# GLU pairs: the low-weight passes of the 64-channel rest as couples of 64-row matmuls

## Chip, cores and metric

The kernel runs on one core of a Trainium2 chip. The metric is the device time of one execution in microseconds (us); before the change it is 1588.62 us, the median of three runs.

## What is computed

A pre-norm block over one sequence of 2048 tokens with 576 channels, all in float32: layer norm, attention with 32 heads of 18 channels in which a token looks at itself and seven earlier tokens at distance 2, an output projection and a residual; then layer norm and a gated linear unit with 4608 hidden channels, and a second residual. The change lies in the gated unit:

```python
S, D, F = 2048, 576, 4608
h = x + attention(layernorm(x), wqkv) @ wo
y = layernorm(h)
g = einsum("bsd,df->bsf", y, w_gate)
u = einsum("bsd,df->bsf", y, w_up)
out = h + einsum("bsf,fd->bsd", sigmoid(g) * u, w_down)
```

## The kernel before

**Numbers in two parts.** Products run in a 32-bit format that TensorE reads with fewer bits (fp32r). So `split` (L104, L105) makes of each operand a high part (a rounded copy by ScalarE) and a low part (the remainder, by VectorE), and a product of 128 input channels is three passes: high weights by high and by low data, low weights by high data.

**576 channels.** They are four blocks of 128 channels and a rest of 64. The rest has tiles of its own, packed twice: the weights of the rest stand in rows 0 to 63 and again in rows 64 to 127. Of the data, rows 0 to 63 hold the high part and rows 64 to 127 the low part (`split_rest`, which subtracts in rows 64 to 127). So one pass with the high weights over 128 rows does high and low data at once; a second pass with the low weights over 128 rows does low weights by high data, and, in the other 64 rows, low by low. `rest` (L612 to L617) issues these two passes.

**Blocks and pairs.** The tokens are four blocks of 512. The 4608 hidden channels are 36 groups of 128. A group is worked out for two token blocks together by `pair`, which takes the gate and up products of both blocks as seven products in place of eight, with sums and differences of the operands (`a00`, `s2`, `s3` and so on for the data, `b00`, `t2`, `t3` and so on for the weights). Each product (`prod`, L603 to L610) covers 256 of the channels: two blocks of 128, three passes each, six matmuls of 128x128 weights by 512 columns. The rest of 64 channels isn't part of that scheme: it is added by four calls of `rest`, to gate and up of each block.

**Banks.** A pair works in three PSUM banks, b1, b2 and b3. Several products go into the same bank one after the other, and in between the bank's content is copied out (`s1`, `s2`, `s3`, by ScalarE) or added to what was copied (by VectorE), which the next product into this bank waits for. The three names rotate from pair to pair over three tiles of 512 columns; the third tile also serves background work (`bg_bank`) outside of the pairs.

**The order of work.** The run over the groups is a list of items: 14 groups singly for the first two token blocks, 22 as pairs, 14 singly for the other two blocks, 36 as pairs. Between the products of a pair, `between(i)` puts in units of the down-projection of earlier groups (`down_units`, L723, in the first pairs; `down_seven`, L785, in the last 36) and steps of background work: attention and projection of the later token blocks in the first pairs, operands for the down-projection in the last. Weights are loaded two groups ahead and split one group ahead (`weights`). A scheduler that knows priorities (`tc.high_priority`) sets the final order on each engine; a matmul can so move past neighbours that it doesn't depend on.

Of the kernel before, what the change touches and what calls it, by code (L numbers as in the profile page):

```python
# [17 lines left out]
AF = mybir.ActivationFunctionType  # L18
ALU = mybir.AluOpType
# [34 lines left out]
HC = 700  # L54
# [6 lines left out]
def kernel(ctx, tc, x, wqkv, wo, wmlp, out):  # L61
    nc = tc.nc
    dve, act, pool, pe, sp = nc.vector, nc.scalar, nc.gpsimd, nc.tensor, nc.sync
# [34 lines left out]
    def f32(ap):  # L98
        return ap.bitcast(F32)
# [3 lines left out]
    def split(hi, lo, src):  # L103
        act.activation(hi, src, AF.Copy)  # L104
        splits.append(dve.tensor_tensor(lo, src, f32(hi), ALU.subtract))  # L105

    def split_rest(t, src):
        act.activation(t, src, AF.Copy)
        dve.tensor_tensor(t[64:128], src[64:128], f32(t[64:128]), ALU.subtract)  # L109

    def pads(g):
        for e in range(2):
# [174 lines left out]
    def th_tile():  # L287
        return xt.tile([P, 5, TB], F32R, tag="th", bufs=3, name="th")

    def tl_tile():  # L290
        return xt.tile([P, 4, TB], F32R, tag="tl", bufs=4, name="tl")

    def x_half(raw, rest):
        t = tl_tile() if rest is None else th_tile()
        split(t[:, 0:2], t[:, 2:4], raw)
        if rest is not None:
            split_rest(t[:, 4], rest)
        return t


# [64 lines left out]
    def qkv_w(g, wr=None):  # L365
        w = saw.tile([P, 2, 5, NQ], F32R, tag="qw", bufs=2, name="qw")
        for c in range(5):
            if wr is None:
                ws = sas.tile([P, NQ], F32, tag="wst", bufs=3, name="ws")
                sp.dma_start(ws, wqkv[g][:, c * NQ:(c + 1) * NQ])  # L370
            else:
                ws = wr[:, c]
            with tc.high_priority(3 * HI if g == 0 else HI):
                split(w[:, 0, c], w[:, 1, c], ws)
        return w
# [63 lines left out]
    w = [qkv_w(0, raw_w(0))]  # L439
# [78 lines left out]
    X = {}  # L518
# [85 lines left out]
    def prod(ps, xx, w, n, first):  # L604
        wt, k0 = w[n]
        k = 0
        for c in range(2):
            for a, m in ((0, 0), (0, 2), (1, 0)):
                pe.matmul(ps, wt[:, a, k0 + c], xx[:, m + c], start=first and k == 0,  # L609
                          stop=k == 5, skip_group_check=True)  # L610
                k += 1

    def rest(ps, xx, w, n):
        wt, k0 = w[n]
        for a in range(2):
            pe.matmul(ps, wt[:, a, k0], xx[:, 4], start=False, stop=a == 1,  # L616
                      skip_group_check=True)  # L617

    gc_bufs = 3

    def halves(name, src):
# [13 lines left out]
    def b_tile(i):  # L635
        return gp.tile([P, TB], F32, name=f"b{i % 3 + 1}")
# [31 lines left out]
    added = [None]  # L668
    gated = [None]

    turn = [2]

    def pair(X, w, between, last):
        turn[0] += 1
        b1, b2, b3 = (b_tile(turn[0] + k) for k in range(3))
        s1, s2, s3 = s_tile(), s_tile(), s_tile()
        prod(b1, X["a00"], w, "b00", True)
        with tc.high_priority(HC):
            act.activation(s1, b1, AF.Copy)
        between(0)  # L680
        prod(b2, X["a01"], w, "b10", True)
        rest(b2, X["a01"], w, "g4")
        with tc.high_priority(HC):
            added[0] = dve.tensor_tensor(s1, s1, b2, ALU.add)
            act.activation(s1, s1, AF.Sigmoid)
        between(1)
        prod(b1, X["s2"], w, "t2", False)
        with tc.high_priority(HC):
            act.activation(s2, b1, AF.Copy)
        between(2)  # L690
        prod(b3, X["s3"], w, "t3", True)
        with tc.high_priority(HC):
            act.activation(s3, b3, AF.Copy)
        between(3)
        prod(b1, X["s1"], w, "t1", False)
        rest(b1, X["a11"], w, "u4")
        with tc.high_priority(HC):
            added[0] = dve.tensor_tensor(s3, s3, b1, ALU.add)  # L698
        between(4)
        prod(b3, X["a11"], w, "t4", False)  # L700
        rest(b3, X["a11"], w, "g4")
        with tc.high_priority(HC):
            added[0] = dve.tensor_tensor(s2, s2, b3, ALU.add)
            gated[0] = act.activation(s2, s2, AF.Sigmoid)
        between(5)
        prod(b1, X["s4"], w, "b11", False)
        rest(b1, X["s4"], w, "u4")
        with tc.high_priority(HC):
            last((s1, b1), (s2, s3))
        between(6)  # L710

# [157 lines left out]
    def operands(pp, p, Xn, names, a0, a1):  # L869
        if p == 0:  # L870
            a0 = pp.tile([P, 5, TB], F32, name="ar0")
            pool.dma_start(a0, xscr[0])
        s = [pp.tile([P, 2, TB], F32, name=f"rs{i}") for i in range(3)]
        rd = pp.tile([P, TB], F32, name="rd")
        if p == 1:
            for n in ("a00", "a01"):
                a = a0[:, 0:2] if n == "a00" else a0[:, 2:4]
                with tc.high_priority(HI):
                    Xn[n] = x_half(a, None if n == "a00" else a0[:, 4])
                yield  # L880
        raw = yield from sums(a0, a1, a1[:, 0:2] if p == 1 else a0[:, 0:2], *s, rd)
        for n in names:
            with tc.high_priority(HI):
                Xn[n] = x_half(*raw[n])
            yield
        return raw

# [15 lines left out]
    Xn = {}  # L903
# [35 lines left out]
    raw = None  # L939
# [170 lines left out]
    for c, (kind, p, f) in enumerate(items):  # L1110
        w, d = wc
        for b, late_c in ((0, NF + NSTD - 3), (1, NF + NSTD + 5)):
            if c == late_c:
                e, hf = BLOCKS[b]
                paced(ov[e, hf], hacc[b])
        skip = () if kind == "std" else (3,)
        by_seven = c >= NF + NSTD
        if c == NSTD:
            finish_bg()
            last_x = splits[-1]  # L1120
            bg = under_rest(getattr(last_x, "ins", last_x))
        if c == NF + NSTD:
            finish_bg()
            with tc.high_priority(HI):
                for n in ("s1", "a11"):
                    Xn[n] = x_half(*raw[n])
            X = Xn
            pp_stk.close()
            dw = ctx.enter_context(sb_pool("dw", "right"))
        if c + 1 < len(items):  # L1130
            wc = weights(items[c + 1][0], wg, c + 1 < NF + NSTD)
        if c + 2 < len(items):
            wg = load_gu(items[c + 2][2], n=WC if c + 2 < NF + NSTD else GU)
        hid = {}
        blocks = [p] if kind == "std" else [2 * p, 2 * p + 1]

        def last(h0, h1):
            hid[0] = hidden(*h0, "h0")
            hid[1] = hidden(*h1, "h1")

        if kind == "std":
            hid = single(X, w, p, late, twice)
        elif not by_seven:
            side = last_pair if c == NF - 1 else bg_step

            def between(i):
                if i in (4, 6):
                    units(2)
                side(i)

            pair(X, w, between, last)
        else:
            def between(i):
                nonlocal st, gc, gc_bufs, dk
                units(1)
                if c == NF + NSTD and i == 5:
                    assert not queue
                    st_stk.close()
                    gc_stk.close()
                    gc = gc_stk.enter_context(sb_pool("gc2"))  # L1160
                    st = st_stk.enter_context(sb_pool("st2"))
                    dk = dk_stk.enter_context(sb_pool("dk", "right"))
                    for n in ("s4h", "s4l", "s1h"):
                        dk.tile([P, TB], F32R, name=n)
                    gc_bufs = 2
                down_side(f, i)

            pair(X, w, between, last if f >= NF - NPL else last_sums(f))
            if f < NF - NPL:
                if f % 2:  # L1170
                    if f == 1:
                        queue.append(lag(LAG))
                    queue.append(seven())
                continue
            d = M[f]
        seg.append((hid, d))
        if len(seg) == 2:
            if by_seven and f == NF - NPL + 1:
                queue.append(load_tails())
            for b in blocks:  # L1180
                queue.append(down_std(seg, b, f // 2) if kind == "std" else
                             down_tail(seg, b, f == NF - 1) if by_seven else down_units(seg, b))
            seg = []
# [44 lines left out]
```

## Time and profile before

| | |
|---|---|
| timed runs, median of 3 | 1588.62 us (1587.64 to 1589.95) |
| profiled execution, first to last instruction | 1589.2 us |
| TensorE matmul busy (PE) | 1553.3 us, 98% |
| TensorE weight loads busy (PEld) | 1381.6 us, 87% |
| VectorE busy (DVE) | 1268.1 us, 80% |
| ScalarE busy (ACT) | 869.2 us, 55% |
| GpSimd busy (POOL) | 184.2 us, 12% |
| mean granted TensorE clock | 0.993 |

The profile is of one execution by itself, with no other time given for it than its span; it lies among the timed runs. Weight loads overlap matmuls, and the end of a matmul is modelled, so busy times of neighbouring matmuls overlap too: what a matmul costs in a dense stretch is read from the start of one to the start of the next. In the rows of the profile, a group has line, engine, operation, tiles written and read, shape (128\*128 is rows by columns of the weights), count, then busy time, mean length of one in ns, and idle time before. A row of the timeline has start, time, engine, line and count, with neighbours of one kind merged.

### The profile page before, as it was taken

What the parts mean: (1) busy time and instruction counts of PE and PEld (TensorE: products, weight loads), DVE (VectorE), ACT (ScalarE), POOL (GpSimd) and SP (SyncE); (2) the same over time, 40 slices, a digit from 0 to 9 for tenths busy, and PEclk for the clock granted to TensorE, in tenths of its full rate; (3) what the DMA queues carried; (4) which work ended last, traced back from release to release, by engine and by line L of the source; (5) the groups of instructions that cost most, each with busy time, mean ns of one, the idle gap of its engine ahead of it and who ended that gap; (6) DMA issues with size and microseconds to landing.
All of it is one profiled execution on the core that took longest, in us unless ns stands there. A gap on an engine that the chain in (4) does not pass through costs nothing.

```text
span 1589.2 us, 22383 instructions
## 1 busy us (share of the span) xinstructions
PE 1553.3 (98%) x8532; PEld 1381.6 (87%) x8532; DVE 1268.1 (80%) x1931; ACT 869.2 (55%) x1546; POOL 184.2 (12%) x230
## 2 busy tenths in 40 slices
PE   7999979999999999999989999999999999999998
PEld 6999968888888888888879988888888888888887
DVE  7999988959999999999546687876677776677755
ACT  4432234425555666656443255776677776677761
POOL 1000000011010001000101100122112112212210
PEclk9999999999999999999999999999999999999999
DMA  7664544346367565665764234899989999989983
GB/s 267 208 206 163 193 184 165 133 177 246 104 164 205 157 170 139 166 191 149 210 203 143 100 110 110 182 186 181 176 169 183 184 173 180 177 170 182 184 170 124
DMA packets 76892, 273.50 MB, mean 172 GB/s; under 512 B 8336, under 2 KB 14224, under 8 KB 75888
## 3 DMA queue, kind: packets, MB, share of 16 engines
q0 software_dynamic: 27792, 105.89, 36.3%
q1 hardware_dynamic: 41360, 146.06, 27.4%
q10 hardware_dynamic: 7632, 20.12, 3.3%
q8 instruction: 67, 1.10, 0.3%
q14 instruction: 41, 0.34, 0.1%
HBM read 145.88 MB, written 128.52 MB: 173 GB/s over the span
## 4 chain that ended last, share of the span: by engine, by line
PE 55%; issue 27%; POOL 7%; DVE 6%; DMA 4%; ACT 1%; SPq 0%; POOLq 0%; ACTq 0%; DVEq 0%
PE b L609 23%; PE dp L723 15%; POOL h L794 7%; PE acc L150 6%; PE b L616 4%; PE b L150 1%; PE bgp L150 1%; DMA wg<-in_wmlp_dram 1%; DVE pr L182 1%; DMA x<-tok 1%; DVE pr L208 1%; DVE lg L186 1%; PE acc L152 1%; DMA tail<-h 1%; PE acc L153 1%
## 5 line engine op out<-in xcount | busy, mean ns | idle before, releaser
L609 PE MATMUL b<-tl,w 128*128 128x512 f32 x1716 | 438.1, 395 | 9.1 <-ACT w L104 6.5
L609 PEld LDWEIGHTS b<-tl,w 128*128 128x128 f32 x1716 | 311.7, 189 | 66.5 <-ACT w L104 7.7
L609 PE MATMUL b<-th,w 128*128 128x512 f32 x1368 | 352.8, 393 | 0.4 <-DVE s L698 0.3
L609 PEld LDWEIGHTS b<-th,w 128*128 128x128 f32 x1368 | 249.8, 188 | 46.7 <-DVE s L698 0.7
L104 ACT ACTIVATE w<-wg 128x640 fp32r<-128x640 f32 (+2 forms) x197 | 117.0, 598 | 125.2 <-PE b L616 59.8
L791 ACT ACTIVATE ev<-dp 128x576 f32<-128x576 f32 x224 | 145.0, 647 | 61.8 <-PE dp L785 58.2
L616 PE MATMUL b<-th,w 128*128 128x512 f32 x572 | 177.0, 391 | 0.0
L794 POOL DMA_DIRECT2D h<-ev x128 | 110.2, 862 | 456.8 <-ACT ev L791 440.5
L105 DVE TENSOR_TENSOR w<-wg,w 128x640 fp32r<-128x640 f32 (+2 forms) x197 | 126.8, 649 | 38.7 <-ACT w L104 38.3
L150 PE MATMUL acc<-qw,th 128*128 128x432 f32 x512 | 155.7, 365 | 1.2 <-DVE th L109 0.9
L105 DVE TENSOR_TENSOR w<-tw,w 128x512 fp32r<-128x512 f32 x116 | 79.6, 687 | 81.1 <-ACT w L104 80.2
L616 PEld LDWEIGHTS b<-th,w 128*128 128x128 f32 x572 | 107.7, 188 | 23.1
L723 PE MATMUL dp<-d,h0h 128*128 128x288 f32 x640 | 119.0, 296 | 1.7 <-DVE tail L733 1.7
L723 PE MATMUL dp<-d,h1h 128*128 128x288 f32 x640 | 120.0, 297 | 0.0
L723 PEld LDWEIGHTS dp<-d,h0h 128*128 128x128 f32 x640 | 99.4, 189 | 5.5 <-DVE tail L733 2.0
L150 PEld LDWEIGHTS acc<-qw,th 128*128 128x128 f32 x512 | 97.2, 190 | 6.5 <-DVE th L109 1.1
L723 PEld LDWEIGHTS dp<-d,h1h 128*128 128x128 f32 x640 | 99.5, 190 | 2.9
L731 ACT ACTIVATE stage<-dp 128x576 f32<-128x576 f32 x96 | 61.7, 646 | 62.4 <-PE dp L723 62.3
L104 ACT ACTIVATE w<-tw 128x512 fp32r<-128x512 f32 x116 | 72.8, 628 | 41.3 <-PE b L609 40.9
L150 PE MATMUL acc<-qw,tl 128*128 128x432 f32 x256 | 92.8, 362 | 0.0
L384 ACT ACTIVATE ev<-acc 128x432 f32<-128x432 f32 x64 | 33.9, 531 | 104.4 <-PE acc L153 97.7
L182 DVE TENSOR_TENSOR pr<-kw,q 128x2304 f32<-128x2304 f32 x32 | 81.7, 2552 | 2.8 <-DMA kw<-k 2.6
(278 smaller groups left out, 2899.8 us busy)
## 6 DMA issues: line engine op xcount, KB each, us to landing
h<-ev POOLq DMA_DIRECT2D x96, 576.0 KB, 7.2
wg<-in_wmlp_dram SPq DMA_DIRECT2D x49, 928.0 KB, 5.2
h<-stage POOLq DMA_DIRECT2D x24, 1152.0 KB, 10.6
wg<-in_wmlp_dram SPq DMA_DIRECT2D x36, 640.0 KB, 4.1
kw<-k SPq DMA_DIRECT2D x16, 792.0 KB, 4.4
vw<-v SPq DMA_DIRECT2D x16, 792.0 KB, 5.5
wd<-in_wmlp_dram SPq DMA_DIRECT2D x18, 576.0 KB, 7.2
h<-ev POOLq DMA_DIRECT2D x32, 288.0 KB, 6.8
```

Of the source, the lines that this page charges most:

```text
L104: act.activation(hi, src, AF.Copy)
L105: splits.append(dve.tensor_tensor(lo, src, f32(hi), ALU.subtract))
L150: pe.matmul(ps[:, :n], a[:, c, js], m[:, c], start=k == 0, stop=False)
L152: pe.matmul(ps[:, :n], th[:, 4, js], wh[:, 4], start=False, stop=False)
L182: dve.tensor_tensor(pr, both(kw, u), q[:, us].unsqueeze(2).broadcast_to([P, 2, W, CG]), ALU.mult)
L384: act.activation(ev[:, :, j], ps[:, :NQ].rearrange("p (t c) -> p t c", t=3), AF.Copy)
L609: pe.matmul(ps, wt[:, a, k0 + c], xx[:, m + c], start=first and k == 0, stop=k == 5, skip_group_check=True)
L616: pe.matmul(ps, wt[:, a, k0], xx[:, 4], start=False, stop=a == 1, skip_group_check=True)
L723: pe.matmul(ps[:, i, :DH2], a[:, js], d[:, m, i * DH2:(i + 1) * DH2], start=k == 0, stop=k == n)
L731: act.activation(hv, ps, AF.Copy)
L791: act.activation(hs[:, k % 2], ps[:, :, :DH2], AF.Copy)
L794: pool.dma_start(hsev[:, u, k0:k + 1], hs[:, :k + 1 - k0], accum_op=ALU.add, max_dma_last_dim=8 * D)
```

## The change

The pass with the low weights needs 64 rows only, those that hold the high part of the data. `rest_two` takes two rests at a time: first the two passes with high weights over 128 rows, then the two passes with low weights, the first on rows 0 to 63 and the second on rows 64 to 127, into different banks. The second of the two always has the operand `a11`: for it the halves of the data are packed the other way round (`low=0`: low part in rows 0 to 63, high part in rows 64 to 127), so that its high part lies in the half that is used. In the second couple the half of rows 0 to 63 is `s4` and that of rows 64 to 127 `a11`.

So that two rests meet, the products of a pair stand in another order, and the four calls become two: gate of the first block with up of the second, and the two remaining ones at the end. The bank b3 is always the third tile now, and b1 and b2 change places from pair to pair.

```diff
-    def split_rest(t, src):
+    def split_rest(t, src, low=1):
         act.activation(t, src, AF.Copy)
-        dve.tensor_tensor(t[64:128], src[64:128], f32(t[64:128]), ALU.subtract)
+        r = slice(64 * low, 64 * low + 64)
+        dve.tensor_tensor(t[r], src[r], f32(t[r]), ALU.subtract)
...
+    def rest_two(top, bot, w):
+        for ps, xx, n in (top, bot):
+            wt, k0 = w[n]
+            pe.matmul(ps, wt[:, 0, k0], xx[:, 4], start=False, stop=False, skip_group_check=True)
+        for i, (ps, xx, n) in enumerate((top, bot)):
+            wt, k0 = w[n]
+            r = slice(64 * i, 64 * i + 64)
+            pe.matmul(ps, wt[r, 1, k0], xx[r, 4], start=False, stop=True, skip_group_check=True)
...
-    turn = [2]
+    turn = [0]
 
     def pair(X, w, between, last):
-        turn[0] += 1
-        b1, b2, b3 = (b_tile(turn[0] + k) for k in range(3))
+        turn[0] = 1 - turn[0]
+        b1, b3, b2 = b_tile(turn[0]), b_tile(2), b_tile(1 - turn[0])
         s1, s2, s3 = s_tile(), s_tile(), s_tile()
         prod(b1, X["a00"], w, "b00", True)
         with tc.high_priority(HC):
             act.activation(s1, b1, AF.Copy)
         between(0)
-        prod(b2, X["a01"], w, "b10", True)
-        rest(b2, X["a01"], w, "g4")
+        prod(b3, X["s3"], w, "t3", True)
         with tc.high_priority(HC):
-            added[0] = dve.tensor_tensor(s1, s1, b2, ALU.add)
-            act.activation(s1, s1, AF.Sigmoid)
+            act.activation(s3, b3, AF.Copy)
         between(1)
         prod(b1, X["s2"], w, "t2", False)
         with tc.high_priority(HC):
             act.activation(s2, b1, AF.Copy)
         between(2)
-        prod(b3, X["s3"], w, "t3", True)
-        with tc.high_priority(HC):
-            act.activation(s3, b3, AF.Copy)
+        prod(b2, X["a01"], w, "b10", True)
         between(3)
         prod(b1, X["s1"], w, "t1", False)
-        rest(b1, X["a11"], w, "u4")
+        rest_two((b2, X["a01"], "g4"), (b1, X["a11"], "u4"), w)
         with tc.high_priority(HC):
             added[0] = dve.tensor_tensor(s3, s3, b1, ALU.add)
+            added[0] = dve.tensor_tensor(s1, s1, b2, ALU.add)
+            act.activation(s1, s1, AF.Sigmoid)
         between(4)
         prod(b3, X["a11"], w, "t4", False)
-        rest(b3, X["a11"], w, "g4")
+        between(5)
+        prod(b1, X["s4"], w, "b11", False)
+        rest_two((b1, X["s4"], "u4"), (b3, X["a11"], "g4"), w)
         with tc.high_priority(HC):
             added[0] = dve.tensor_tensor(s2, s2, b3, ALU.add)
             gated[0] = act.activation(s2, s2, AF.Sigmoid)
-        between(5)
-        prod(b1, X["s4"], w, "b11", False)
-        rest(b1, X["s4"], w, "u4")
-        with tc.high_priority(HC):
             last((s1, b1), (s2, s3))
         between(6)
```

More of the change, by code (lines that the diff above doesn't have):

```diff
@@ L291, in tl_tile, with x_half @@
         return xt.tile([P, 4, TB], F32R, tag="tl", bufs=4, name="tl")
-    def x_half(raw, rest):
+    def x_half(raw, rest, low=1):
         t = tl_tile() if rest is None else th_tile()
@@ L296, in x_half @@
         if rest is not None:
-            split_rest(t[:, 4], rest)
+            split_rest(t[:, 4], rest, low)
         return t
@@ L883, in operands @@
             with tc.high_priority(HI):
-                Xn[n] = x_half(*raw[n])
+                Xn[n] = x_half(*raw[n], n != "a11")
             yield
@@ L1125 @@
                 for n in ("s1", "a11"):
-                    Xn[n] = x_half(*raw[n])
+                    Xn[n] = x_half(*raw[n], n != "a11")
             X = Xn
```

## The prediction

> **What bounds the kernel now.** I read the page first, then the stages, the waits of TensorE, the groups by shape, and two short stretches of the timeline.
>
> ```profile
> span 1589.2 us, 22383 instructions
> PE 1553.3 (98%) x8532; PEld 1381.6 (87%) x8532; DVE 1268.1 (80%) x1931; ACT 869.2 (55%) x1546; POOL 184.2 (12%) x230
> ...
> 420.00:700.00 280.00, 280.00 (x1544) 248.01 (x1543) 272.15 (x344) 164.90 (x269) 23.18 (x22) 1.00 0.63 166
> 960.00:1540.00 580.00, 580.00 (x3112) 507.14 (x3112) 423.83 (x732) 408.56 (x720) 110.54 (x128) 1.00 0.88 175
> ...
> PE mm L139 <- DVE tok L134: 9.5, 2, 9.1
> PE b L609 <- ACT w L104: 6.5, 1, 6.5
> ```
>
> The two rows of windows lie in the two stretches of GLU pairs (the first pairs with attention beside them, then the last 36 pairs). The columns are busy time and instructions of PE, PEld, DVE, ACT and POOL, then granted clock, DMA share and GB/s. PE is busy for every microsecond of both, at clock 1.00, and its largest waits in the whole run are 9.5 and 6.5 us. So the pairs cost what their matmuls cost, one after the other, and a pass that is saved is time that is saved, as long as nothing else becomes late. Two things stand near: DVE, with 272.15 of 280 us (97%) in the first stretch, and the DMA engines at 0.88 in the second.
>
> A busy PE can hide gaps, because a matmul's end is modelled. The pitch, start to start, cannot:
>
> ```profile
> L616 PE MATMUL b<-th,w 128*128 128x512 f32 x572 | 177.0, 391 | 0.0
> ...
> 1005.68 0.85 PE L609 MATMUL b<-th,w 128*128 128x512 f32 x3
> 1006.14 0.41 PEld L616 LDWEIGHTS b<-th,w 128*128 128x128 f32 x2
> 1006.37 0.62 PE L616 MATMUL b<-th,w 128*128 128x512 f32 x2
> 1006.60 0.19 PEld L785 LDWEIGHTS dp<-d,h1h 128*128 128x128 f32 x1
> 1006.82 0.29 PE L785 MATMUL dp<-d,h1h 128*128 128x288 f32 x1
> ```
>
> L616 is `rest`: each call issues a high and a low pass. Three passes of L609 take 1006.37 - 1005.68 = 0.69 us, or 0.23 each; the two of L616 take 0.45 until L785 starts. The group says the same over the whole run: its 572 passes are 286 neighbours, whose covered time is 177.0/286 = 0.619 us; less the 0.391 of the second one, the first took **0.228 us** before the second began. The rest of the 0.391, **0.163 us**, is the modelled way of the last column through the array after the next matmul has begun. The weight load of each pass starts when the matmul before it starts (1006.60 is 1006.37 + 0.23), and is covered.
>
> **What the change takes away.** There are 22 + 36 = 58 pairs. Each had four `rest` calls, eight passes of 128 rows. Now the four high passes stay, and the four low passes become two couples of 64-row passes: 116 couples. In the built order of the instructions 115 of them stand side by side; the 116th, in the first pair, is split by the scheduler. No matmul count changes, so without overlap inside a couple nothing is gained. With it, a couple that cost 2 x 0.228 = 0.456 us costs one stream of 512 columns plus the lag of its second member.
>
> That lag is not in the trace, which has no matmul of 64 rows (every form is 128*128). It is bounded by zero below and by a bare weight load above. The nearest row for a bare load are the transposes, whose streams are so short that loads set their pitch:
>
> ```profile
> 870.00 0.62 PE L616 MATMUL b<-th,w 128*128 128x512 f32 x2
> 870.46 0.27 PE L143 MATMUL bgp<-ident,oj 128*128 128x128 f32 x1
> 870.57 0.60 PE L139 MATMUL b<-ident,oj 128*128 128x128 f32 x4
> 870.92 0.50 PE L723 MATMUL dp<-d,h1h 128*128 128x288 f32 x2
> ...
> 870.46 0.47 PEld L139 LDWEIGHTS b<-ident,oj 128*128 128x128 f32 x4
> ```
>
> Four loads in 0.47 us and four matmuls in 0.60 us, one matmul being 0.27: (0.60 - 0.27)/3 = **0.11 us** a load. I take the upper end, 0.11, because every load in the trace starts with the matmul ahead of it and none earlier: the second half's load would start with the first half's matmul and its stream 0.11 later. A couple then costs 0.228 + 0.11 = 0.338, saves 0.118, and 115 of them save 115 x 0.118 = **13.6 us**. The lower end, no lag, saves 115 x 0.228 = 26.2 us.
>
> The other unknown is what it costs to go from 128-row to 64-row passes and back, 2 x 115 = 230 times. The nearest row here is the change from products to transposes and back in the same lines: 870.46 - 870.00 = 0.46 for two passes, the ordinary pitch, and L723 starts 0.35 after the first of four transposes (870.92 - 870.57), where three loads alone take 0.33. So that change of kind shows no gap. It is no change of rows, however. I take zero, and keep 0.163, the whole tail, as the other end. The Trainium skill speaks against zero: its page "TensorEngine Tiling (Array Packing)", section Tiling Modes, says that changing the tiling mode, and not just the tile, drains TensorE; the same list says that tiles load weights and multiply in parallel. No run here shows either. By the first, the sum is that of the drain below.
>
> **What the reordering moves.** The products now run b00, t3, t2, b10, t1, couple, t4, b11, couple. What must hide is what lay between a product and the next one into the same bank. All rows here are from a pair with attention beside it.
>
> ```profile
> 503.23 0.62 PE L616 MATMUL b<-th,w 128*128 128x512 f32 x2
> 503.68 0.42 PE L723 MATMUL dp<-d,h0h 128*128 128x288 f32 x2
> 506.87 1.54 PE L609 MATMUL b<-tl,w 128*128 128x512 f32 x6
> 508.11 2.55 DVE L182 TENSOR_TENSOR pr<-kw,q 128x2304 f32<-128x2304 f32 x1
> 508.25 1.52 PE L609 MATMUL b<-th,w 128*128 128x512 f32 x6
> 508.51 0.60 ACT L679 ACTIVATE s<-b 128x512 f32<-128x512 f32 x1 [0.79 <-PE b L609]
> 509.61 0.62 PE L616 MATMUL b<-th,w 128*128 128x512 f32 x2
> 510.06 4.24 PE L609 MATMUL b<-tl,w 128*128 128x512 f32 x18
> 510.58 0.68 DVE L684 TENSOR_TENSOR s<-s,b 128x512 f32<-128x512 f32 x1
> ```
>
> - The copy of b1 (L679) ends at 509.11, and t2 wrote b1 again at 510.06: 0.95 us to spare. The two rest passes no longer lie between, 0.45 us; 0.5 us is left. Cost nothing; without that cover, ScalarE's order would show it as a wait of PE on `act` at t2.
> - b3 is now read by the last addition of a pair, and written again by the second product of the next. Between lie two down-projection units, 506.87 - 503.68 = 3.19 us, and b00, 1.38: 4.57 us, against one attention operation of 2.55 ahead of an addition of 0.68, 3.23 together. Nothing.
> - b1's addition before b11 has two units and t4 between, the same 4.57 us. Nothing.
> - The second sigmoid now comes after the pair's end, so the second hidden product is later by about an addition and an activation (0.68 + 0.60 from the rows above). Its reader, a down-projection, stands in the next pair. Nothing. The weight splits stay one pair ahead, and DVE, ACT and DMA do the same work as before. No DMA issue passes another, since none is in the part that is reordered.
>
> **The sum.** The profiled execution, 1589.2 us from first to last instruction, would take 1589.2 - 13.6 = 1575.6; the median of the timed runs is 1588.62, 0.6 lower, so 1588.6 - 13.6 = **1575.0 us**. What this kernel's measurement can tell from no change is about 0.2%, 3.2 us.
>
> **The rivals.**
>
> *The change of rows empties the array (slower).* Each of the two changes of a couple adds the tail of 0.163. With the lag of 0.11 a couple then saves 0.118 and pays 0.326: +0.208 x 115 = +23.9 us, **1612.5**. Without lag: 0.326 - 0.228 = +0.098, +11.3 us, 1599.9. Were the weights of the next pass also held until the array is empty, two bare loads of 0.11 come on top of each: +0.318 x 115 = +36.6 us (1625.2) without lag, +0.428 x 115 = +49.2 us (1637.8) with it. It decides from a gap of 0.059 us a change with lag, of 0.114 without. For it: nothing in this kernel has made TensorE change rows, and the tail of 0.163 is there to be exposed. Against: the transposes go in and out without a gap, but they are another kind of change. I give it 0.42, of which 0.24 for the tail alone. The Trainium skill's drain rule ("TensorEngine Tiling (Array Packing)", Tiling Modes) would have it so, without a price.
>
> *Both halves start together.* Saves 26.2 us, **1562.4**. For it: the second load writes rows that the first doesn't, and two loads at 0.11 fit into the 0.228 of the pass before. Against: no load in the trace starts two matmuls ahead. The Trainium skill, "TensorE: Matmul & The Clock Gate", Part 3, says loads for other row groups are pulled ahead and tile matmuls start about 4 ns apart; no run here shows that yet. In the stretch with attention it would come near DVE's limit: two couples save 0.456 us of a pair's 50 x 0.228 + 2 x 3.19 = 17.8 us, 2.6%, and DVE has 3% left. Chance 0.22.
>
> *The halves do not overlap, or overlap just pays for the change.* The count of passes is as before, and the time stays **1588.6**, within 3.2 us. For it: no trace here shows two matmuls at once. Chance 0.08.
>
> **How the numbers follow.** My forecast, overlap with a lagging second half and at most a small gap, has 0.28. Faster by over 0.2%: 0.28 + 0.22 = 0.50. Within 0.2%: 0.08. Slower: 0.42. The likeliest group alone, faster, spans 1562 to 1585 (a gap up to 0.045 us a change leaves 3 us of the 13.6). The range for 8 in 10 must cross to the drain: from 1562 to 1626, which holds the tail alone and the held weights without lag, and leaves out those with lag, somewhat above 0.1.
>
> **What would show it.** Rows of 64*128 at the `rest_two` lines should number 232. In a couple the second should start 0.11 after the first (0.00 in the second rival, 0.23 in the third), and the next full pass 0.23 after the second. A first half that starts 0.39 or more after the full pass ahead of it, or a full pass that late behind a couple, is the drain. A pair of the last stretch should be shorter by 0.24 us. Waits of PE on `act` at t2 or on `dve` at t3 would make the third part wrong. The prediction is wrong if the time is not below 1585.

## The result: slower by 1.25%, and the profile after

The changed kernel takes **1611.09 us** (median of 4 runs, 1607.72 to 1611.51) against 1589.28 us before (4 runs), a ratio of **1.0125** with a 95% interval of 1.0113 to 1.0137. The forecast was 1575.0, faster. The profiled execution of the changed kernel is the quickest of its four, 1607.72 us with a span of 1605.4; the spans of the others are 1608.8 to 1609.3.

The stages and TensorE's waits of the kernel after, in the same views as before:

```profile
420.00:700.00 280.00, 280.00 (x1514) 234.77 (x1513) 271.31 (x341) 162.32 (x266) 23.15 (x22) 1.00 0.64 166
960.00:1540.00 580.00, 580.00 (x3055) 479.35 (x3055) 423.25 (x720) 391.12 (x705) 107.60 (x125) 1.00 0.85 171
...
PE mm L140 <- DVE tok L135: 9.4, 2, 8.9
PE b L610 <- ACT w L104: 6.7, 1, 6.7
```

PE is busy all through both stretches, at clock 1.00, and waits for nothing new. Yet it issues 1514 matmuls in 280 us where it issued 1544, and 3055 in 580 us where it issued 3112: 1.9% and 1.8% fewer. So the loss lies in the pairs, evenly, and inside TensorE; the busy time of PE doesn't show it, the count does.

The groups of the two lines of `rest_two`, and one couple in the timeline (PE first, then its weight loads):

```profile
L623 PE MATMUL b<-th,w 128*128 128x512 f32 x232 | 71.6, 389 | 0.0
L627 PE MATMUL b<-th,w 64*128 64x512 f32 x232 | 58.6, 498 | 0.0
...
1020.16 0.61 PE L623 MATMUL b<-th,w 128*128 128x512 f32 x2
1020.71 0.50 PE L627 MATMUL b<-th,w 64*128 64x512 f32 x2
1021.14 0.40 PE L791 MATMUL dp<-d,h0h 128*128 128x288 f32 x1
1021.37 0.29 PE L791 MATMUL dp<-d,h0l 128*128 128x288 f32 x1
...
1019.94 0.41 PEld L623 LDWEIGHTS b<-th,w 128*128 128x128 f32 x2
1020.70 0.19 PEld L627 LDWEIGHTS b<-th,w 64*128 64x128 f32 x2 [0.35 <-issue]
1021.13 0.19 PEld L791 LDWEIGHTS dp<-d,h0h 128*128 128x128 f32 x1 [0.24 <-issue]
```

This is read row by row, with 0.228 us as the length of a stream of 512 columns:

- **Both halves run at once.** Two matmuls of 64 rows stand in one row of 0.50 us; one alone has 0.498. They start within 0.01 us of each other, so the lag of 0.11 that the forecast took isn't there.
- **A gap on the way in.** The second high pass starts at 1020.16 + 0.61 - 0.39 = 1020.38 and the couple at 1020.71, 0.32 to 0.33 later: its stream and 0.09.
- **A bare weight load.** The couple's loads start with it (1020.70), not with the pass ahead of it, where every load stood before. A matmul of 64 rows therefore has 498 ns where one of 128 rows has 389: 0.109 of it is waiting for weights.
- **A gap on the way out.** The next full pass starts 1021.14 - 1020.71 = 0.43 after the couple: 0.109 for the weights, 0.228, and 0.09 again.
- **A second bare load.** That pass too starts with its load (1021.13): it has 0.40 us, where its neighbours of the same form have 0.29, and the one behind it comes 0.23 later, where 0.13 is usual.

A couple thus pays 0.09 + 0.11 + 0.09 + 0.11, some **0.40 us for the trip** to 64 rows and back, and saves one stream, 0.228. The trace has finer times: at the median of the 115 couples the next full pass starts 0.749 us after the second high pass. Less the high pass's own 0.227, and with the 0.107 for the load behind, a couple costs 0.629, where two streams cost 0.454: a balance of +0.175 us. 115 couples make 20.1 us, and the two halves that the scheduler parted, each a trip by itself, 0.8. That is 20.9 of the 21.8 us lost. The two profiled spans differ by 16.2 us only, 1605.4 against 1589.2: in this quickest run the listed waits of PE add up to 27.7 us, 3.9 less than the 31.6 before.

### The profile page after: what moved, and what is told of

The parts are those of the page before. It is cut to its first block, busy times and chain, and to the rows that moved or that the text cites. A ratio compares the mean times of both kernels' runs of the same rounds, so it can differ in the third digit from the quotient of the medians.

```text
span 1605.4 us, 22371 instructions
## 1 busy us (share of the span) xinstructions
PE 1573.4 (98%) x8532; PEld 1349.1 (84%) x8532; DVE 1275.4 (79%) x1931; ACT 856.6 (53%) x1546; POOL 184.0 (11%) x230
## 4 chain that ended last, share of the span: by engine, by line
PE 90%; DVE 4%; DMA 3%; issue 2%; ACT 0%; SPq 0%; POOL 0%; ACTq 0%; POOLq 0%; DVEq 0%
PE b L610 44%; PE dp L729 16%; PE dp L791 12%; PE acc L151 6%; PE b L623 3%; PE b L627 3%; PE b L617 1%; DMA wg<-in_wmlp_dram 1%; PE b L151 1%; PE bgp L151 1%; DVE pr L209 1%; DVE pr L183 1%; DVE lg L187 1%; PE acc L153 0%; PE b L140 0%
## 5 line engine op out<-in xcount | busy, mean ns | idle before, releaser
L610 PE MATMUL b<-th,w 128*128 128x512 f32 x1368 | 349.5, 393 | 0.0
L610 PEld LDWEIGHTS b<-th,w 128*128 128x128 f32 x1368 | 249.5, 188 | 47.4 <-issue 1.2
L104 ACT ACTIVATE w<-wg 128x384 fp32r<-128x384 f32 (+2 forms) x197 | 111.8, 598 | 176.1 <-PE b L627 84.2
L105 DVE TENSOR_TENSOR w<-wg,w 128x384 fp32r<-128x384 f32 (+2 forms) x197 | 126.4, 648 | 37.7 <-ACT w L104 37.6
L706 ACT ACTIVATE s<-s 128x512 f32<-128x512 f32 x58 | 36.6, 631 | 109.0 <-DVE s L705 108.9
L705 DVE TENSOR_TENSOR s<-s,b 128x512 f32<-128x512 f32 x58 | 39.7, 684 | 63.4 <-PE b L627 63.1
```

## Experiments

Six kernels, all made from the changed one, were run beside the kernel before (1590.2 us, the median of 15 and of 11 runs).

**The order alone.** The low passes go over 128 rows again; order, banks and packing stay new.

```diff
-            r = slice(64 * i, 64 * i + 64)
+            r = slice(0, 128)
```

> The changed kernel with its new order of products, banks and packing, but the two low passes of rest_two over 128 rows again, so no matmul of 64 rows. Theory: all of the loss lies in the couples, 115 times (0.629 - 2 x 0.227) = 0.175 us and two split passes at 0.4 us, 20.9 us of the 21.8 us lost; the order alone then costs nothing, and this runs in 1589 us within 3, with no pitch over 0.24 at the rest passes. Rival: the new order made some bank, copy or addition late, and the couples only part of the loss; then this stays well above 1592, up to 1611, with waits of PE on ScalarE or VectorE.

Measured: 1591.18 us, ratio 1.0008 (0.9999 to 1.0017). The order costs about 1 us, at most 2.7 by the interval; PE's waits are nearly those of before, with a new one of 1.0 us on an addition (L704). The windows of the middle of the last stretch say the same, for the kernel before, the new order alone, and the changed kernel:

```profile
1000.00:1500.00 500.00, 500.00 (x2699) 437.85 (x2698) 363.81 (x632) 357.72 (x630) 100.46 (x117) 1.00 0.91 179
...
1000.00:1500.00 500.00, 500.00 (x2694) 437.15 (x2693) 365.46 (x631) 347.89 (x627) 100.14 (x117) 1.00 0.90 179
...
1000.00:1500.00 500.00, 500.00 (x2647) 414.16 (x2646) 368.00 (x631) 343.05 (x620) 97.98 (x114) 1.00 0.88 175
```

In these 500 us there are 2699, 2694 and 2647 matmuls. The loss is the couples'.

**One couple a pair.** The first of the two is two full passes again.

```diff
-    def rest_two(top, bot, w):
+    def rest_two(top, bot, w, full=False):
...
-            r = slice(64 * i, 64 * i + 64)
+            r = slice(0, 128) if full else slice(64 * i, 64 * i + 64)
...
-        rest_two((b2, X["a01"], "g4"), (b1, X["a11"], "u4"), w)
+        rest_two((b2, X["a01"], "g4"), (b1, X["a11"], "u4"), w, True)
```

> The changed kernel with the first couple of each pair as two full passes of 128 rows; the second stays a couple of 64-row passes. Theory: each couple costs 0.175 us more than two full passes wherever it stands, so 58 of them cost 10.2 us: 1599.5 us, half the loss. Rival (the order, not the couples): 1611, as before. A second rival (a first couple costs more than a second, because one of its halves waits for VectorE): under 1598 or over 1602.

Measured: 1602.77 us, ratio 1.0080 (1.0067 to 1.0094), which is 12.6 us over before, and 11.6 over the order alone. Half the couples cost a little over half of the loss; per couple 0.20 where 0.175 was expected. It misses the theory's 1599.5 and lies just within the second rival's range. But with the 1 us of the order the theory gives 1591.2 + 10.2 = 1601.4, which lies inside the interval of the ratio (1600.8 to 1605.1), so the extra 1.4 us are no evidence for that rival. That the loss goes with the number of couples holds; the rival of the order, at 1611, falls.

**Both passes on the same half.** Rows 0 to 63 for both, and all operands packed as before.

```diff
-            r = slice(64 * i, 64 * i + 64)
+            r = slice(0, 64)
...
-                Xn[n] = x_half(*raw[n], n != "a11")
+                Xn[n] = x_half(*raw[n])
```

> The changed kernel with both passes of a couple on rows 0 to 63, one after the other, and all operands packed as in the kernel before. Theory: going to 64 rows and back costs 0.40 us a time, made of two gaps of 0.09 and two bare weight loads of 0.107, and the overlap of the halves gives 0.227 back; without the overlap a couple costs 0.85 us, so 115 x 0.227 = 26 us more than the changed kernel, 1637 us, with 0.227 from the first of a couple to the second. Rival (the halves only start together and do not run together, so the couple is slow because each takes its own time): no longer than the changed kernel, 1611 us.

Measured: 1635.57 us, ratio 1.0287 (1.0271 to 1.0303), 24.5 us over the changed kernel. From the first of a couple to the second it is not the expected 0.227, though, but 0.73 - 0.39 = 0.34 us in the rows below: the first waits for its weights, 0.11, and then streams. The second has 0.39 us, like a full pass; its own load is hidden.

**Each couple twice.**

```diff
-        for i, (ps, xx, n) in enumerate((top, bot)):
+        for i, (ps, xx, n) in ((0, top), (1, bot), (0, top), (1, bot)):
```

> The changed kernel with each couple issued twice in a row, so that four passes of 64 rows stand together; the low weights' part is added twice, so the sum is another one. Theory: what is dear is going there and back, and a second couple in the same place costs one stream, 0.227 us, its weights loaded under the first: 115 x 0.23 = 26 us more than the changed kernel, 1637 us. Rival (each couple pays its own gaps and bare loads, because loads do not go under matmuls of 64 rows or the two halves must both end): 0.4 to 0.63 us a couple, 46 to 72 us more, 1657 to 1683 us.

Measured: 1636.97 us, ratio 1.0295 (1.0281 to 1.0309), 25.9 us over the changed kernel. This experiment and the one before it belong together. First the shortest, median and longest time of the passes on one half, in ns; then one trip of each in the timeline, with two passes on one half and with four passes on both halves, and the loads of the latter:

```profile
L627 PE MATMUL b<-th,w x232: 392/493/498, 393.3 to 1602.8; 64*128 64x512 f32 x116
...
1033.46 0.73 PE L627 MATMUL b<-th,w 64*128 64x512 f32 x2
1034.11 0.40 PE L791 MATMUL dp<-d,h0h 128*128 128x288 f32 x1
...
1022.98 0.73 PE L627 MATMUL b<-th,w 64*128 64x512 f32 x4
1023.64 0.40 PE L791 MATMUL dp<-d,s3h 128*128 128x288 f32 x1
...
1022.98 0.30 PEld L627 LDWEIGHTS b<-th,w 64*128 64x128 f32 x4 [0.35 <-issue]
1023.64 0.19 PEld L791 LDWEIGHTS dp<-d,s3h 128*128 128x128 f32 x1 [0.36 <-issue]
```

Two passes on one half take as long as four on both, 0.73 us, and the next full pass comes 0.65 to 0.66 after the first. So the overlap of the halves is whole, and worth a stream: without it, 24.5/115 = 0.21 us more. And a second couple in the same trip costs 25.9/115 = 0.225 (0.73 - 0.50 = 0.23 in the rows), one stream and nothing else: its loads lie under the first couple, and no gap stands between couples. What is dear is going there and back.

**A unit between.** A down-projection unit, into other banks, stands between the high passes and the first couple.

```diff
+        apart()
         for i, (ps, xx, n) in enumerate((top, bot)):
...
-        rest_two((b2, X["a01"], "g4"), (b1, X["a11"], "u4"), w)
+        rest_two((b2, X["a01"], "g4"), (b1, X["a11"], "u4"), w, lambda: between(4))
...
-        between(4)
```

> The changed kernel with a unit of the down-projection, which writes other banks, between the two high passes and the first couple of a pair. Theory: the gap at the way in belongs to the change of rows, so it stays 0.09 after a matmul of 288 columns that writes another bank (0.22 from start to start against 0.13 as usual), and the time stays at 1611 us, plus 0.62 us for each of 11 couples more that the scheduler splits, about 1618. Rival (the gap is a wait for the bank that the high pass has just written): the way in shows 0.13 there, and 58 x 0.09 = 5 us are won back, about 1613 with the same split couples.

Measured: 1623.33 us, ratio 1.0205 (1.0191 to 1.0218). The timeline ahead of a couple:

```profile
1031.27 0.29 PE L791 MATMUL dp<-d,h0l 128*128 128x288 f32 x1
1031.40 0.29 PE L791 MATMUL dp<-d,h0h 128*128 128x288 f32 x1
1031.62 0.49 PE L628 MATMUL b<-th,w 64*128 64x512 f32 x2
```

Where 0.13 us is usual from one matmul of 288 columns to the next, the couple comes 0.22 after the last of them: the same gap of 0.09, behind another bank. The rival, a wait for the bank, falls, and nothing is won back. The time is 5 us over what was expected. PE's list has one wait of 2.2 us on an addition (L705) that the changed kernel's list doesn't have; where the rest lies was not followed up.

**Two couples in one trip.** All four low passes stand at the end of the pair, with a fourth bank in the rotation (short form):

```diff
-        b1, b3, b2 = b_tile(turn[0]), b_tile(2), b_tile(1 - turn[0])
+        b1, b2, b3 = (four_tile(turn[0] + k) for k in range(3))
...
-        rest_two((b1, X["s4"], "u4"), (b3, X["a11"], "g4"), w)
+        rest_high(((b1, X["s4"], "u4"), (b3, X["a11"], "g4")), w)
+        rest_low(((b1, X["s4"], "u4"), (b3, X["a11"], "g4"),
+                  (b2, X["a01"], "g4"), (b3, X["a11"], "u4")), w)
         with tc.high_priority(HC):
+            added[0] = dve.tensor_tensor(s1, s1, b2, ALU.add)
+            act.activation(s1, s1, AF.Sigmoid)
```

> All four low passes of a pair stand together at its end, as two couples in one trip to 64 rows, with a fourth bank for the pair's rotation and the first gate's addition moved behind them. One of the four (low weights of the second block's up part) goes into another bank than it belongs to, since its own has been read by then, so the sum is another one; this is a price, not a version. Theory: a trip costs 0.40 us, each couple gives 0.227 back, so two couples in one trip gain 0.055 us a pair, 58 x 0.055 = 3.2 us, less about 1 us for the order: 1587 to 1590 us, level with the kernel before within 3. Within a trip 0.00, 0.33, 0.00 from start to start, and 0.32 to the next full pass. Rival (the trip grows with the passes in it, or the addition at the end becomes late for the next pair): over 1594 us.

Measured: 1602.84 us (6 runs), ratio 1.0079 (1.0066 to 1.0093). The forecast missed; the run's profile tells the price of a trip from what else went wrong. Here are the window in the last stretch, the two waits of PE that are longer than any other kernel's in the pairs, the products right behind the first of them with the window there, and twelve passes of a product elsewhere in the same run:

```profile
1000.00:1500.00 500.00, 500.00 (x2699) 422.54 (x2698) 373.45 (x635) 347.78 (x630) 99.74 (x116) 1.00 0.89 179
...
PE b L610 <- DVE s L718: 3.9, 1, 3.9
PE bgp L610 <- ACT s L702: 3.6, 1, 3.6
...
422.63 5.32 PE L610 MATMUL b<-tl,w 128*128 128x512 f32 x12 [3.92 <-DVE s L718]
423.00:428.00 5.00, 5.00 (x13) 3.87 (x13) 4.96 (x10) 3.02 (x7) 0.00 (x0) 0.53 0.53 189
...
469.84 2.90 PE L610 MATMUL b<-th,w 128*128 128x512 f32 x12
```

With one trip of two couples a pair, the dense stretch runs exactly as before, 2699 matmuls in 500 us. The gain of 0.055 us a pair would be 9 matmuls there; against the order alone, with 2694, 5 of them are seen. Over the 57 whole trips, the mean from the last high pass to the next full pass is 0.986 us; less 0.227, and with 0.107 for the load behind, that is 0.866 against 0.908 for four streams, a gain of 0.04 a pair, 2.4 us in all. The loss comes from two single waits, 7.5 us: one for the addition that now comes last, early in the first stretch, one for a copy near the end. Behind the first, the granted clock is 0.53 from 423 to 428 us, and twelve passes take 5.32 us in place of 2.90, another 2.4. That is 9.9 us lost and 2.4 gained, where 9.2 lie between the spans (1598.4 against 1589.2); of what is left, the order alone had 1.2 (1590.4). So the rival of a late addition was right, but once and not in each pair. The profiled run is the second quickest of the six; what the slower ones lost more isn't known. Even a version without these waits would only be about level, and this one still has one pass in a wrong bank; no version that beats the kernel before came out of these runs.

## Why the prediction was wrong, point by point

- **What bounds the kernel:** right. PE stays dense, and every 0.1 us of its pitch counts at once, 116 times.
- **The reordering costs nothing:** right, about 1 us (1591.18 against 1590.2). The slack of the banks was enough.
- **The lag of the second half, taken as 0.11:** wrong, it is under 0.01. The weights of both halves are loaded in the same 0.11. The Trainium skill's sentence that tile matmuls start about 4 ns apart ("TensorE: Matmul & The Clock Gate", Part 3) agrees with the trace; the order of loads among full passes was no guide to half ones. Taken alone this would have made the gain larger. At the change of rows, however, no load was pulled ahead: the couple's loads start with the couple (1020.70).
- **The change of rows, taken as free:** this is the step that failed. "I take zero" rested on the transposes, which go in and out without a gap but use all 128 rows. The runs show 0.09 us for the change itself and 0.11 for the first load behind it, at each of the 230 changes: 0.40 us a couple, where the overlap gives 0.228. The Trainium skill's rule that a change of tiling mode drains TensorE ("TensorEngine Tiling (Array Packing)", Tiling Modes) was cited against the forecast, and the trace agrees with it: the gap stands at each change, behind any bank, and not between couples. It names no price. What holds the start for 0.09 us, an array that empties or something else, no run tells apart.
- **The weights on either side:** the rival had them, "held until the array is empty", as its dear variant without lag: +36.6 us, where the runs show 20.9. The loads do come late, as it said (that the array must be empty for them isn't shown); the term too large was the gap, 0.09 and not the modelled tail of 0.163. Two gaps alone would have left a gain, 0.228 - 0.18 = 0.05 us a couple. It is the two bare loads, 0.22, that turn the sign. The row of the transposes had a sign of such a load: the two passes of L723 behind them take 0.50 us, where two take 0.42 elsewhere (503.68), although the forecast read no gap there.
- **The rival's 1612.5,** for the tail alone with lag, lies 1.4 us from the measured time by chance: 2 x 0.163 + 0.11 - 0.228 = 0.208 is near 0.175, but with other terms.
- **Chances and range:** the measured time is inside the range because it reached to the drain. The sign was given 0.50 for faster with nothing in the trace that showed two halves at once or a change of rows for nothing; between a rule that speaks of a drain and a row of another kind, the row got too much.

## What to carry to other kernels

Count the trips to another number of rows, not the passes: here a trip costs 0.40 us, and each couple of 64-row passes gives back one stream, 0.23 us, so a trip with one couple loses and one with two is about level, by its rows and not by its measured time. Before packing half-height matmuls between full ones, see how many can stand side by side; here the number of banks that can be held open limits it. In a stretch where TensorE is busy throughout, count its matmuls per microsecond; here its busy time stayed at 100% with the gaps and without.

## What the runs showed of the hardware that was not expected

- Matmuls on rows 0 to 63 and 64 to 127, into different banks, overlap wholly in fp32r: four in the time of two (0.73 us).
- Going from 128 to 64 rows, and back, costs 0.09 us each here, and the first weight load after each change isn't taken ahead: another 0.11 each.
- Inside a trip neither is paid: a further couple adds 0.225 us, with its loads hidden.
